# Closing attention's buffer pools one stage earlier, and making the block products' input sums there

## The chip, the cores and the metric

The kernel runs on one core of a Trainium2 chip. The metric is the device time of one execution in microseconds (us), as the median over several executions. The engines are TensorE (PE, with its weight loads listed as PEld), VectorE (DVE), ScalarE (ACT), GpSimd (POOL) and SyncE (SP), which issues nearly all DMAs.

## The reference

Three stages follow each other. q, k, v have shape (4, 12, 448, 64): four batches, twelve heads.

```python
q_n, k_n = rmsnorm(q, g_q), rmsnorm(k, g_k)
attn = softmax(q_n @ k_n.T / 8)          # per batch and head, 448 x 448
x = (attn @ v)                           # as 1792 tokens x 768
h = x @ moe_w_in;  g = s * relu(h)**2 + b;  x = g @ moe_w_out      # 768 -> 2048 -> 768
h = x @ moe2_w_in; out = (h * cos(h)) @ moe2_w_out                 # 768 -> 2048 -> 768
```

The weights of the first layer come as float64 and the result is float32, so the products are made in three passes from pairs of a high and a low part.

## The kernel before

**Tiling.** A matrix is held as a pair: `high` is a cast to fp32r made by ACT, `low` is the remainder, one subtraction made by DVE or POOL. Each product is three matmuls: high by high, high by low, low by high (`products`, L138). A batch is 448 columns. The hidden dimension of 2048 is cut into eight chunks of two 128-row tiles.

**Order of the work.** The two feed-forward layers are one list of units, made at L887 to L925. An `in` unit makes one 128 x 448 tile of h (18 matmuls) and its activation; an `out` unit adds one chunk's share to one output tile (6 matmuls), after which DVE adds it to the accumulator (L801), or ACT copies it at a tile's first visit (L799). The first layer goes through segments: 0 and 2 are chunk 0 for batch 0 and for batch 1, 1 is chunks 1 to 7 for batches 0 and 1, and 3 (the second pass) is all eight chunks for batches 2 and 3. Segment 4 is the second layer. A generator, `attention` (L149), is advanced between the units by a planner of costs (L1003 to L1008). A scheduler then orders each engine's queue: earlier in the program goes first among what it takes to be ready, and only written dependences bind. `issue_after` (L107) fixes an order in a queue without a wait, `follow` (L103) is a wait.

**Block products.** From chunk 2 of segment 3 on, the `in` work of a chunk is one unit `seven` (L668): seven products of half size in place of eight. It needs sums of blocks of the inputs (t1 to t4) and of the weights (`load_combined`, L588). For each of three columns c, `fetch_x` (L621) reads four 128 x 448 pieces of attention's result back from DRAM, and `combine_x` (L628) makes four differences on DVE (L630 to L633), four high casts on ACT (L636) and four low parts on DVE (L637). They stand in segment 3: fetches behind its 1st, 3rd and 5th following unit, sums behind the 4th, 6th and 9th (L988 and L989). The first fetch of each column follows a high cast of a recent `in` unit (L626), and the first difference is queued behind a recent activation on DVE (L630).

**Memory.** Attention has an SBUF pool `att` and a PSUM pool `ps` of six banks (`sc` four, `tp` two); two more banks, tag `mo`, are the feed-forward's own. At the end of segment 2 (L980 to L987) `att` and `ps` are closed and their room goes to `xb` (the second home of inputs), `mb` (among others eight buffers `acc`) and the PSUM pool `psb` (three banks `ph` for `in`, three banks `po` for `out`). Until then `in` units take `mo` and `out` units take `mo`, or `sc` once all pairs are finished (`po_tile`, L775). `fetch` (L860) reads batch 3 back into six tiles of `att`.

**Names of time.** The change's point is the unit `in` of segment 1, chunk 7, tile 0, batch 1. Counted from it: 0 and 1 are that `in` and the next, 3 and 4 the two `in` units of segment 2, 5 to 16 the `out` units of chunk 7, 17 to 22 those of segment 2, 23 is the border to segment 3, 24 to 29 are six `in` units, and 30 is its first `out`.

Of the kernel before, what the change touches and what calls it, by code (L numbers as in the profile page):

```python
# [10 lines left out]
F32 = mybir.dt.float32  # L11
# [4 lines left out]
ALU = mybir.AluOpType  # L16
AX = mybir.AxisListType
PSUM = bass.MemoryType.PSUM
# [25 lines left out]
def body(ctx, tc, q, k, v, g_q, g_k, w1_in, w1_out, s_in, b_in, w2_in, w2_out, out):  # L44
# [23 lines left out]
    LOOK = 8  # L68
    TAIL = 14
    NEAR = 4  # L70
    AHEAD = 3, 5
    SEVEN = 2

    const = ctx.enter_context(tc.tile_pool(name="const", bufs=1))
    dram = ctx.enter_context(tc.tile_pool(name="dram", bufs=1, space=DRAM))
# [544 lines left out]

    def fetch_x(c):  # L621
        x11, x12, x21, x22 = mixed["raw", c] = [pools["mb"].tile([P, E], F32, tag="acc", name=f"xc_{c}_{n}", bufs=2 * NT - NE)[:, :S] for n in range(4)]
        for n, (t, b, cc) in enumerate(((x11, 2, c), (x12, 3, c), (x22, 3, c + NE // 2), (x21, 2, c + NE // 2))):
            dma = nc.sync.dma_start(t, stash[0, b, cc])
            if n == 0:
                follow(dma, marks["gh"])  # L626

    def combine_x(c):  # L628
        x11, x12, x21, x22 = mixed.pop(("raw", c))
        issue_after(nc.vector.tensor_tensor(x11, x12, x11, ALU.subtract), marks["sums"])  # L630
        nc.vector.tensor_tensor(x12, x22, x12, ALU.subtract)
        nc.vector.tensor_tensor(x22, x22, x11, ALU.subtract)
        nc.vector.tensor_tensor(x21, x21, x22, ALU.subtract)  # L633
        for n, (name, t) in enumerate((("t1", x11), ("t3", x12), ("t2", x22), ("t4", x21))):
            hi, lo = mixed[name, c] = [z[:, n // 2 * S:(n // 2 + 1) * S] for z in held_x["b"][c + n % 2 * (NE // 2)]]
# [8 lines left out]
    def g_pair(key, seg):  # L644
        n = count["pairs"] % (5 if seg > 3 else 4)
        count["pairs"] += 1
        if "mb" not in pools or n < 3:
            gp, tag, nb = ma, "g", 3
        else:
            gp, tag, nb = pools["mb"], "gx"[n - 3], 1  # L650
        return [gp.tile([P, 2 * S], F32R, tag=tag + z, name=f"g{z}_{key}", bufs=nb) for z in "hl"]

    def squared(h, key, place=None):
        def temp(pool, tag, name):
            return pool.tile([P, WIDE], F32, tag=tag, name=f"{name}_{key}")[:, :h.shape[1]]

        r = temp(ma, "t0", "r") if place is None else place
        nc.scalar.activation(r, h, AF.Relu)
        r2 = temp(pools["mb"], "t1", "r2") if "mb" in pools else r
# [5 lines left out]
        marks["sums"] = nc.vector.tensor_scalar(gt, r2, sb[:, 0:1], sb[:, 1:2], ALU.mult, ALU.add)  # L665
        return gt

    def unit_seven(layer, seg, ck, *_):  # L668
# [115 lines left out]
    def unit_out_1(seg, ck, et, b):  # L784
# [73 lines left out]
    early = {}  # L858

    def fetch(b):  # L860
        for c in range(NP):
            t = pools["att"].tile([P, S], F32, tag=("xf", "qT", "kT")[c % 3], name=f"xe_{b}_{c}")
            nc.sync.dma_start(t, stash[0, b, c])
            early[0, b, c] = t

    def behind_weights(high, low, eng):
        near = [z for z in casts if z[0] <= count["unit"] + NEAR]
# [71 lines left out]

    def lead(z):  # L940
        n, key = z
        return n - AHEAD[key[1] > SEVEN] if key[0] == "s" else n

    todo.sort(key=lead)

# [19 lines left out]
    enter = [units.index(("next", seg)) for seg in range(1, L2 + 1)]  # L965
    last = {max(n for n, u in enumerate(units) if u[:3] == ("in", 0, 1) and u[5] == 0): 2, enter[2] - TAIL: 3}
    rates = [1.05 * PAIR * (2 * NP - ALONE) / spent(units[:enter[0]]), 1.05 * PAIR * 2 * NP / spent(units[enter[0]:max(last)])]
    debt = 0.0
    seg = 0
    soon, again = [], []  # L970
    fetches, sums = {}, {}
    wait = 0
    for n, u in enumerate(units):
        count["unit"] = n
        ahead(n + LOOK)
        if u[0] == "next":
            seg = u[1]
            if seg == 1:
                until(2)
            if seg == 3:  # L980
                for _ in steps:
                    pass
                att_scope.close()
                pools["xb"] = ctx.enter_context(tc.tile_pool(name="xb", bufs=1))
                held_x["b"] = paired(pools["xb"], "b")
                pools["mb"] = ctx.enter_context(tc.tile_pool(name="mb", bufs=2))
                pools["psb"] = ctx.enter_context(tc.tile_pool(name="psb", bufs=2, space=PSUM))  # L987
# [14 lines left out]
        for cost in {"in": unit_in, "seven": unit_seven, "out": unit_out}[u[0]](*u[1:]):  # L1002
            debt += cost * rates[min(seg, 1)]  # L1003
            while debt > 0:
# [1 line left out]
                if c is None:  # L1006
                    break
                debt -= c  # L1008
        if n in fetches:
            fetch_x(fetches[n])  # L1010
        if n in sums:
            combine_x(sums[n])
# [36 lines left out]
```

## Time and profile before

| what | value |
|---|---|
| median of 3 executions | 1248.81 us (1247.53 to 1249.16) |
| profiled execution, its own time | 1248.98 us |
| its span, first to last instruction | 1247.2 us |
| mean granted TensorE clock | 0.998 |
| PE, DVE, ACT, POOL busy | 98%, 72%, 62%, 49% |

A row of the waits says which engine sat idle, for which instruction, and what ended the idle time. In a timeline the idle time before an instruction and its releaser stand in brackets at the end of its row. Matmuls overlap their neighbours, so their starts tell the pace: products of 448 columns follow each other by about 0.2 us.

### The profile page before, as it was taken

Reading aid. Unit: us, or ns where it says so; the run is one execution under the profiler, and the core shown is the slowest. Engines: PE = TensorE matmul, PEld = TensorE weight load, DVE = VectorE, ACT = ScalarE, POOL = GpSimd, SP = SyncE. Lnnn points to the kernel's source line nnn. Section 1 sums busy time; section 2 is a strip of 40 time slices with the busy share of each in tenths; the row PEclk is TensorE's granted clock in tenths of the full one; section 3 lists DMA queues with packets and bytes.
Section 4 is the critical chain, followed back from the end, with each engine's and each line's share of the span. In section 5 each row is a group of like instructions: output and inputs, shape, how many; then the busy total and the mean of one; then the engine's idle time right before and its main releaser. Section 6 shows DMA issues by size and latency. Waiting matters only on the chain.

```text
span 1247.2 us, 18906 instructions
## 1 busy us (share of the span) xinstructions
PE 1220.1 (98%) x6575; PEld 1032.8 (83%) x6575; DVE 893.5 (72%) x1510; ACT 777.6 (62%) x1725; POOL 608.3 (49%) x724
## 2 busy tenths in 40 slices
PE   7999999999999999999999999999999999999998
PEld 5555777777777877888898988899999999999997
DVE  6888778767768664758777778575777666676765
ACT  4788888776666663536445446698666756565640
POOL 4777647464544524734333333556444635363541
PEclk9999999999999999999999999999999999999999
DMA  4334336344333333443212241131111111111105
GB/s 119 96 106 119 106 97 196 111 134 132 116 114 106 113 122 121 158 155 93 58 51 69 78 139 42 36 114 52 52 51 52 51 52 51 51 52 51 55 10 177
DMA packets 88463, 114.08 MB, mean 91 GB/s; under 512 B 11952, under 2 KB 78512, under 8 KB 88368
## 3 DMA queue, kind: packets, MB, share of 16 engines
q1 hardware_dynamic: 88048, 112.66, 29.7%
q8 instruction: 51, 0.84, 0.3%
q14 instruction: 44, 0.36, 0.1%
q10 hardware_dynamic: 320, 0.23, 0.1%
HBM read 89.26 MB, written 23.59 MB: 90 GB/s over the span
## 4 chain that ended last, share of the span: by engine, by line
PE 71%; DVE 5%; ACT 2%; DMA 2%; issue 1%; POOL 1%; SPq 0%; DVEq 0%; ACTq 0%; POOLq 0%
PE ph L741 25%; PE po L819 18%; PE po L793 14%; PE av L407 3%; PE tp L372 3%; PE ph_s L685 3%; PE sc L320 3%; PE ph_a L685 2%; DMA t<-wd 1%; DVE xlb L127 0%; DVE xlb L637 0%; DVE acc L801 0%; ACT wh L535 0%; PE rt L391 0%; DVE wl L538 0%
## 5 line engine op out<-in xcount | busy, mean ns | idle before, releaser
L765 POOL TENSOR_TENSOR gl<-gt,gh 128x512 fp32r<-128x512 f32 (+1 forms) x104 | 126.6, 1228 | 119.4 <-ACT gh L764 119.2
L538 POOL TENSOR_TENSOR wl<-t,wh 128x384 fp32r<-128x384 f32 x128 | 140.3, 1112 | 90.1 <-ACT wh L535 82.6
L741 PE MATMUL ph<-xha,wh 128*128 128x448 f32 (+2 forms) x432 | 159.6, 370 | 1.5 <-DVE acc L801 0.8
L741 PE MATMUL ph<-xha,wl 128*128 128x448 f32 (+2 forms) x432 | 158.2, 366 | 0.0
L741 PE MATMUL ph<-xla,wh 128*128 128x448 f32 (+2 forms) x432 | 157.5, 366 | 0.0
L819 PE MATMUL po<-wh,gh 128*128 128x384 f32 x448 | 151.9, 340 | 1.3 <-DVE acc L827 1.3
L827 DVE TENSOR_TENSOR acc<-po,acc 128x384 f32<-128x384 f32 x196 | 105.5, 551 | 64.9 <-PE po L819 64.6
L819 PE MATMUL po<-wh,gl 128*128 128x384 f32 x448 | 150.0, 335 | 0.0
L819 PE MATMUL po<-wl,gh 128*128 128x384 f32 x448 | 149.5, 335 | 0.0
L801 DVE TENSOR_TENSOR acc<-po,acc 128x448 f32<-128x448 f32 (+2 forms) x168 | 102.0, 618 | 49.7 <-PE po L793 48.9
L763 POOL TENSOR_TENSOR gt<-hs,gt 128x512 f32<-128x512 f32 x64 | 76.8, 1206 | 119.2 <-ACT gt L762 118.8
L535 ACT CAST wh<-t 128x384 fp32r<-128x384 f32 x176 | 84.2, 512 | 70.6 <-PE po L793 27.5
L579 DVE SCALAR_TENSOR_TENSOR t<-c,t 128x384 uint32<-128x384 uint32 x128 | 96.4, 755 | 40.2 <-ACT t L573 36.8
L347 ACT ACTIVATE pr<-sc,top 128x448 f32<-128x448 f32 x161 | 102.3, 640 | 17.0 <-DVE top L335 16.4
L335 DVE TENSOR_REDUCE top<-sc 128x1 f32<-128x448 f32 x168 | 98.3, 616 | 15.7 <-PE sc L320 14.9
L572 ACT ACTIVATE c<-raw 128x384 f32<-128x384 f32 x128 | 71.2, 558 | 52.3 <-DMA raw<-in_moe_w_in_dram 17.3
L793 PE MATMUL po<-gh,wh 128*128 128x448 f32 (+1 forms) x240 | 91.7, 387 | 6.8 <-DVE acc L801 3.7
L372 PE MATMUL tp<-ident,pr 128*112 128x128 f32 x672 | 95.3, 278 | 1.1 <-DVE pT L384 0.5
L372 PEld LDWEIGHTS tp<-ident,pr 128*112 128x112 f32 x672 | 74.6, 134 | 24.9 <-issue 13.3
L764 ACT CAST gh<-gt 128x512 fp32r<-128x512 f32 (+1 forms) x104 | 57.8, 567 | 56.5 <-DVE gt L665 29.1
L741 PEld LDWEIGHTS ph<-xha,wh 128*128 128x128 f32 x432 | 81.1, 188 | 13.0 <-issue 2.2
L819 PEld LDWEIGHTS po<-wh,gh 128*128 128x128 f32 x448 | 84.1, 188 | 8.9 <-DVE acc L827 6.0
(181 smaller groups left out, 3161.7 us busy)
## 6 DMA issues: line engine op xcount, KB each, us to landing
raw<-in_moe_w_in_dram SPq DMA_DIRECT2D x64, 384.0 KB, 3.6
raw<-in_moe_w_out_dram SPq DMA_DIRECT2D x64, 384.0 KB, 3.3
wd<-t SPq DMA_DIRECT2D x64, 192.0 KB, 2.7
t<-wd SPq DMA_DIRECT2D x48, 192.0 KB, 2.4
rawk<-in_k_dram SPq DMA_DIRECT2D x24, 224.0 KB, 2.9
rawv<-in_v_dram SPq DMA_DIRECT2D x24, 224.0 KB, 3.1
rs<-wd SPq DMA_DIRECT2D x24, 192.0 KB, 2.7
rawq<-in_q_dram SPq DMA_DIRECT2D x23, 192.0 KB, 2.9
```

Source lines behind the costliest of these rows:

```text
L335: line("DVE", nc.vector.tensor_reduce(top, st[i]["sc", c][j][1][:, :S], axis=AX.X, op=ALU.max, negate=True))
L347: e = line("ACT", nc.scalar.activation(pr, sc[:, :S], AF.Exp, bias=st[i]["top"][:, at], scale=scale, accum_out=st[i]["sums"][:, at]))
L372: mm = [nc.tensor.transpose(tp[:, kc * P:(kc + 1) * P], pr[:, kc * CP:(kc + 1) * CP], ident) for kc in range(NCH)]
L535: z = nc.scalar.copy(wh, w)
L538: casts.append((count["needed"], z, eng, eng.tensor_tensor(wl, w, wh.bitcast(F32), ALU.subtract)))
L579: nc.vector.scalar_tensor_tensor(t, c, 0x80000000, t, ALU.bitwise_and, ALU.bitwise_or)
L741: nc.tensor.matmul(h, a, m, start=(c == 0 and n == 0), stop=(c == NE - 1 and n == 2))
L765: nc.gpsimd.tensor_tensor(gl, gt, gh.bitcast(F32), ALU.subtract)
L793: marks["out"] = nc.tensor.matmul(po, a, m, start=(f == 0 and n == 0), stop=(f == CF - 1 and n == 2))
L801: nc.vector.tensor_tensor(at, po, at, ALU.add)
L819: nc.tensor.matmul(po, a, m, start=(f == 0 and n == 0), stop=(f == CF - 1 and n == 2))
L827: nc.vector.tensor_tensor(at, po, at, ALU.add)
```

## The change

Both pools are closed in front of unit 0 instead of at the border to segment 3. `fetch` reads batch 3 into three wide tiles of `mb`. `combine_x` is split into `sums_x` (differences and high casts) and `lows_x` (low parts, two of four now on POOL), and the three steps of column c come behind the units in `PREPARE`, counted from the change's point. The wait of the first fetch on a high cast goes. The order mark is also set by each accumulation. The weight sums of chunk 2 are asked for five units ahead instead of three. Pairs of g before segment 3 stay in their old pool.

```diff
-    AHEAD = 3, 5
+    AHEAD = 5
+    PREPARE = (0, 3, 6), (1, 10, 14), (16, 25, 27)
...
     def fetch_x(c):
...
-            dma = nc.sync.dma_start(t, stash[0, b, cc])
-            if n == 0:
-                follow(dma, marks["gh"])
-    def combine_x(c):
-        x11, x12, x21, x22 = mixed.pop(("raw", c))
-        issue_after(nc.vector.tensor_tensor(x11, x12, x11, ALU.subtract), marks["sums"])
+            nc.sync.dma_start(t, stash[0, b, cc])
+    def sums_x(c):
+        x11, x12, x21, x22 = mixed["raw", c]
+        issue_after(nc.vector.tensor_tensor(x11, x12, x11, ALU.subtract), marks["DVE"])
...
             nc.scalar.copy(hi, t)
-            nc.vector.tensor_tensor(lo, t, hi.bitcast(F32), ALU.subtract)
+    def lows_x(c):
+        x11, x12, x21, x22 = mixed.pop(("raw", c))
+        for n, (name, t) in enumerate((("t1", x11), ("t3", x12), ("t2", x22), ("t4", x21))):
+            hi, lo = mixed[name, c]
+            z = (nc.vector if n % 2 else nc.gpsimd).tensor_tensor(lo, t, hi.bitcast(F32), ALU.subtract)
+            if n == 1:
+                issue_after(z, marks["DVE"])
...
-        nc.vector.tensor_tensor(at, po, at, ALU.add)
+        marks["DVE"] = nc.vector.tensor_tensor(at, po, at, ALU.add)
...
     def fetch(b):
-            t = pools["att"].tile([P, S], F32, tag=("xf", "qT", "kT")[c % 3], name=f"xe_{b}_{c}")
+        for n, tag in enumerate(("xh", "xl", "gh")):
+            t = pools["mb"].tile([P, 2 * S], F32, tag=tag, name=f"xe_{b}_{n}", bufs=1)
...
+    change = units.index(("in", 0, 1, NCK - 1, 0, 1))
...
-            if seg == 3:
-                for _ in steps:
-                    pass
-                att_scope.close()
...
-                fetches = {n + 1: 0, n + 3: 1, n + 5: 2}
-                sums = {n + 4: 0, n + 6: 1, n + 9: 2}
+        if n == change:
+            until(B)
+            for _ in steps:
+                pass
+            att_scope.close()
+            pools["xb"] = ctx.enter_context(tc.tile_pool(name="xb", bufs=1))
...
+        for step, c in prepare.get(n, ()):
+            step(c)
```

## Rows read from the trace of the kernel before

**Rows 1.** The page: busy time by engine, and the chain by engine.
```profile
PE 1220.1 (98%) x6575; PEld 1032.8 (83%) x6575; DVE 893.5 (72%) x1510; ACT 777.6 (62%) x1725; POOL 608.3 (49%) x724
PE 71%; DVE 5%; ACT 2%; DMA 2%; issue 1%; POOL 1%; SPq 0%; DVEq 0%; ACTq 0%; POOLq 0%
```
**Rows 2.** Waits of PE, 490 to 600 us: total, times, longest.
```profile
PE po L793 <- ACT acc L799: 2.5, 3, 1.5
...
PE po L793 <- DVE acc L801: 0.6, 1, 0.6
```
**Rows 3.** PE's timeline around the change: start, us, instruction, idle before.
```profile
487.75 3.23 PE L407 MATMUL av<-pT,rawv 112*64 112x448 f32 x16
...
500.49 0.36 PE L741 MATMUL ph<-xha,wh 128*128 128x448 f32 x1
...
538.84 0.44 PE L741 MATMUL ph<-xha,wh 128*128 128x448 f32 x1 [0.81 <-DVE acc L801]
...
571.14 0.47 PE L793 MATMUL po<-gh,wh 128*128 128x448 f32 x1 [1.48 <-ACT acc L799]
...
613.71 0.44 PE L793 MATMUL po<-gh,wh 128*128 128x384 f32 x1 [1.51 <-DVE acc L801]
```
**Rows 4.** ACT's timeline at the longest of those waits.
```profile
564.65 0.56 ACT L636 CAST xhb<-xc 128x448 fp32r<-128x448 f32 x1 [2.13 <-DVE xc L633]
565.12 0.53 ACT L799 COPY acc<-po 128x448 f32<-128x448 f32 x1
...
570.09 0.56 ACT L636 CAST xhb<-xc 128x448 fp32r<-128x448 f32 x1 [0.79 <-DVE xc L632]
570.56 0.53 ACT L799 COPY acc<-po 128x448 f32<-128x448 f32 x1
```
**Rows 5.** Stretches: length, then busy time of PE, PEld, DVE, ACT, POOL.
```profile
516.00:538.84 22.84, 21.43 (x106) 19.12 (x104) 18.45 (x29) 8.86 (x20) 13.86 (x12) 1.00 0.60 198
538.84:561.10 22.26, 22.26 (x109) 20.15 (x110) 10.48 (x17) 7.66 (x16) 9.43 (x9) 1.00 0.41 128
...
529.86:543.51 13.65, 12.84 (x64) 11.52 (x63) 7.45 (x14) 3.33 (x7) 0.01 (x2) 1.00 0.60 206
```
**Rows 6.** Groups by shape, 538.84 to 588.3 us: busy, mean ns, idle before.
```profile
L637 DVE TENSOR_TENSOR xlb<-xc,xhb 128x448 fp32r<-128x448 f32 x12 | 9.5, 803 | 0.0
...
L632 DVE TENSOR_TENSOR xc<-xc,xc 128x448 f32<-128x448 f32 x3 | 4.2, 1409 | 0.1
L631 DVE TENSOR_TENSOR xc<-xc,xc 128x448 f32<-128x448 f32 x3 | 2.8, 944 | 0.0
L633 DVE TENSOR_TENSOR xc<-xc,xc 128x448 f32<-128x448 f32 x3 | 2.5, 850 | 0.0
...
L630 DVE TENSOR_TENSOR xc<-xc,xc 128x448 f32<-128x448 f32 x3 | 1.8, 613 | 0.0
...
L636 ACT CAST xhb<-xc 128x448 fp32r<-128x448 f32 x12 | 6.8, 568 | 5.1 <-DVE xc L632 2.3 <-DVE xc L633 2.1 <-DVE xc L631 0.6
```
**Rows 7.** DVE's timeline: accumulations ahead of unit 0, an activation behind unit 3.
```profile
497.85 3.46 DVE L801 TENSOR_TENSOR acc<-po,acc 128x448 f32<-128x448 f32 x6 [4.79 <-PE po L793]
...
516.39 1.33 DVE L665 TENSOR_SCALAR gt<-r,sb 128x448 f32<-128x448 f32 x1 [0.83 <-POOL r L661]
```
**Rows 8.** Groups of DVE, 516 to 538.84 us: low parts of weights.
```profile
L538 DVE TENSOR_TENSOR wl<-t,wh 128x384 fp32r<-128x384 f32 x9 | 6.7, 785 | 0.9 <-ACT wh L535 0.9
```
**Rows 9.** POOL's low parts of batch 3, 500.49 to 538.84 us.
```profile
L127 POOL TENSOR_TENSOR xla<-xe,xha 128x448 fp32r<-128x448 f32 x6 | 7.6, 1289 | 0.0
```
**Rows 10.** The twelve reads of attention's result: the line's DMA.
```profile
DMA to landing us min/median/max: 2.5/3.3/5.2
```
**Rows 11.** Timelines of DVE and POOL at the first differences.
```profile
559.41 0.61 DVE L631 TENSOR_TENSOR xc<-xc,xc 128x448 f32<-128x448 f32 x1
560.06 1.47 DVE L632 TENSOR_TENSOR xc<-xc,xc 128x448 f32<-128x448 f32 x1
...
559.16 1.88 POOL L765 TENSOR_TENSOR gl<-gt,gh 128x448 fp32r<-128x448 f32 x1 [1.98 <-ACT gh L764]
```

More of the change, by code (lines that the diff above doesn't have):

```diff
@@ L622, in fetch_x @@
         x11, x12, x21, x22 = mixed["raw", c] = [pools["mb"].tile([P, E], F32, tag="acc", name=f"xc_{c}_{n}", bufs=2 * NT - NE)[:, :S] for n in range(4)]
-        for n, (t, b, cc) in enumerate(((x11, 2, c), (x12, 3, c), (x22, 3, c + NE // 2), (x21, 2, c + NE // 2))):
-            dma = nc.sync.dma_start(t, stash[0, b, cc])
-            if n == 0:
-                follow(dma, marks["gh"])
-    def combine_x(c):
-        x11, x12, x21, x22 = mixed.pop(("raw", c))
-        issue_after(nc.vector.tensor_tensor(x11, x12, x11, ALU.subtract), marks["sums"])
+        for t, b, cc in (((x11, 2, c), (x12, 3, c), (x22, 3, c + NE // 2), (x21, 2, c + NE // 2))):
+            nc.sync.dma_start(t, stash[0, b, cc])
+    def sums_x(c):
+        x11, x12, x21, x22 = mixed["raw", c]
+        issue_after(nc.vector.tensor_tensor(x11, x12, x11, ALU.subtract), marks["DVE"])
         nc.vector.tensor_tensor(x12, x22, x12, ALU.subtract)
@@ L634, in combine_x @@
         for n, (name, t) in enumerate((("t1", x11), ("t3", x12), ("t2", x22), ("t4", x21))):
-            hi, lo = mixed[name, c] = [z[:, n // 2 * S:(n // 2 + 1) * S] for z in held_x["b"][c + n % 2 * (NE // 2)]]
+            hi, _ = mixed[name, c] = [z[:, n // 2 * S:(n // 2 + 1) * S] for z in held_x["b"][c + n % 2 * (NE // 2)]]
             nc.scalar.copy(hi, t)
-            nc.vector.tensor_tensor(lo, t, hi.bitcast(F32), ALU.subtract)
+    def lows_x(c):
[5 more added lines that the diff above has]
+                issue_after(z, marks["DVE"])
     g = {}
@@ L646, in g_pair @@
         count["pairs"] += 1
-        if "mb" not in pools or n < 3:
+        if seg < 3:
+            n = 0
+        if n < 3:
             gp, tag, nb = ma, "g", 3
@@ L664, in squared @@
         gt = temp(ma, "t2", "gt")
-        marks["sums"] = nc.vector.tensor_scalar(gt, r2, sb[:, 0:1], sb[:, 1:2], ALU.mult, ALU.add)
+        marks["DVE"] = nc.vector.tensor_scalar(gt, r2, sb[:, 0:1], sb[:, 1:2], ALU.mult, ALU.add)
         return gt
@@ L860, in fetch @@
     def fetch(b):
-        for c in range(NP):
-            t = pools["att"].tile([P, S], F32, tag=("xf", "qT", "kT")[c % 3], name=f"xe_{b}_{c}")
-            nc.sync.dma_start(t, stash[0, b, c])
-            early[0, b, c] = t
+        for n, tag in enumerate(("xh", "xl", "gh")):
+            t = pools["mb"].tile([P, 2 * S], F32, tag=tag, name=f"xe_{b}_{n}", bufs=1)
+            for c in (2 * n, 2 * n + 1):
+                at = t[:, c % 2 * S:(c % 2 + 1) * S]
+                nc.sync.dma_start(at, stash[0, b, c])
+                early[0, b, c] = at
     def behind_weights(high, low, eng):
@@ L941, in lead @@
         n, key = z
-        return n - AHEAD[key[1] > SEVEN] if key[0] == "s" else n
+        return n - AHEAD if key[0] == "s" else n
     todo.sort(key=lead)
@@ L967, in body @@
     rates = [1.05 * PAIR * (2 * NP - ALONE) / spent(units[:enter[0]]), 1.05 * PAIR * 2 * NP / spent(units[enter[0]:max(last)])]
+    change = units.index(("in", 0, 1, NCK - 1, 0, 1))
+    prepare = {}
+    for c, times in enumerate(PREPARE):
+        for step, at in zip((fetch_x, sums_x, lows_x), times):
+            prepare.setdefault(change + at, []).append((step, c))
     debt = 0.0
@@ L970, in body @@
     soon, again = [], []
-    fetches, sums = {}, {}
     wait = 0
@@ L979, in body @@
                 until(2)
-            if seg == 3:
-                for _ in steps:
-                    pass
-                att_scope.close()
[L984 to L987, printed above, removed]
-                fetches = {n + 1: 0, n + 3: 1, n + 5: 2}
-                sums = {n + 4: 0, n + 6: 1, n + 9: 2}
-            continue
+            continue
+        if n == change:
[4 more added lines that the diff above has]
+            pools["xb"] = ctx.enter_context(tc.tile_pool(name="xb", bufs=1))
+            held_x["b"] = paired(pools["xb"], "b")
+            pools["mb"] = ctx.enter_context(tc.tile_pool(name="mb", bufs=2))
+            pools["psb"] = ctx.enter_context(tc.tile_pool(name="psb", bufs=2, space=PSUM))
         if wait:
@@ L1008, in body @@
                 debt -= c
[L1009 to L1012, printed above, removed]
+        for step, c in prepare.get(n, ()):
+            step(c)
         if u[0] == "seven" and u[3] == NCK - 1:
```

## The prediction, made before the changed kernel was run

> **What bounds the kernel now.** I read the page first, then PE's waits around the change, the timelines at those waits, and a table of stretches. PE is busy in 1220.1 us of a span of 1247.2 us and carries 71% of the chain that ends last [rows 1]. So a gain can only come out of PE's 27 us of idle time, and a loss is new idle time. Between 490 and 600 us the waits of PE that the change could touch are few: 2.5 us in three waits for ACT's copies of a first visit, 0.6 us once for an accumulation on DVE [rows 2], and 0.81 us in front of the first `in` of segment 3 at 538.84 us [rows 3]. Another 1.51 us stands at 613.71 us [rows 3]. Nothing behind that belongs to the sums.
>
> The 2.5 us have a cause that the reader can see in ACT's queue. The copy at 565.12 us, which gives a PSUM bank back to PE, is queued behind a high cast of a sum that had waited 2.13 us for a difference on DVE. At 570.56 us it is the same: the cast ahead had waited 0.79 us [rows 4]. PE's longest wait, 1.48 us, ends right behind that second copy, at 571.14 us [rows 3]. So the input sums, where they stand now, hold PE up by way of ACT's order.
>
> **The change part by part.** The sum is made against the profiled execution, whose own time is 1248.98 us (span 1247.2 us and 1.8 us around it); the median of three is 1248.81 us, 0.2 us less, so I carry the difference over to the median.
>
> *The pools close at unit 0.* Attention is not in the way: its last product starts at 487.75 us and takes 3.23 us, and unit 0 starts at 500.49 us [rows 3]. Nothing is left to drain, so running the generator dry costs nothing; if pairs were left there, their sixteen products alone would cost 3.2 us each. But the new PSUM pool takes the room of banks that the last `out` units still use. Before, the first tile of that pool waited 0.81 us at 538.84 us, until the last accumulation was done [rows 3]. That wait goes, and its like comes at unit 0: six accumulations run from 497.85 to 501.31 us [rows 7], and the tile that now starts at 500.49 us would start at 501.31 us at the earliest, +0.8 us. If the bank in question is free sooner, it is nothing. The wait at 538.84 us is the nearest row, so I take +0.8 us and keep 0.
>
> *Columns 0 and 1 move into the `out` units.* Their first difference is queued behind the activation of unit 3, which DVE makes at 516.39 us [rows 7], so this work lies where DVE gives PE its banks back. In 516.00 to 538.84 us, DVE is busy 18.45 us of 22.84 us and PE 21.43 us [rows 5]. What is added on DVE is eight differences and four low parts. At the shortest of them, 0.61 us [rows 6], that is 7.4 us. At the means, the four differences have 0.61, 0.94, 1.41 and 0.85 us, 3.8 us a column, and two low parts 2 x 0.80 us [rows 6]: 5.4 us a column and 10.8 us in all. What need not be done before the last `out` product: three accumulations, since three banks of the new pool can stay full (3.46 / 6 = 0.58 us each [rows 7], 1.7 us); column 1's low parts, which the block products read only after 577 us; and low parts of weights that segment 3 uses, two of the nine at 0.78 us [rows 8], 1.6 us.
>
> Bounds: PE's own 21.43 us if DVE never holds it up, which is 1.4 us less than now (it contains the waits of 0.60 and 0.81 us). With all twelve at their means and only the accumulations put off, 18.45 + 10.8 - 1.7 = 27.6 us, 4.7 us more. I take column 0 at its mean, 5.4 us, because POOL works through all of its 13.86 us before 529.86 us, and column 1's four differences short, 2.4 us, because POOL then is idle (0.01 us of 13.65 us [rows 5]); one of the two weight parts, 0.8 us, is put off: 18.45 + 7.8 - 1.7 - 0.8 = 23.75 us, +0.9 us.
>
> The long rows decide this term. A difference took 1.47 us while POOL made a low part, yet the one ahead of it, under the same POOL instruction, took 0.61 us [rows 11]; so POOL's work stretches some of them. The Trainium skill, "SBUF — State Buffer", section "Who interferes with whom", has a rule that speaks against this change: a DVE instruction with two SBUF inputs and a GpSimd instruction that reads SBUF contend, and the second to issue blocks fully. By that rule, with the 1.41 us of L632 for all six of column 0, the term would be 3.1 us larger and the sum +2.3 us; the trace agrees in one of the two rows and not in the other.
>
> *The old place is emptied.* In 538.84 to 588.3 us eight of twelve casts, 0.57 us each, and all but four differences and two low parts leave ACT and DVE [rows 6]. Column 2 stays, but its differences now come behind unit 25 and its low parts behind unit 27, where DVE is busy 10.48 us of 22.26 us [rows 5]: 5.4 us fit. If that cover were gone, one cast wait of 0.79 us as in rows 4 would come back. I take -2.5 us for the three waits; the other end is -0.8 us, if two thirds of it stay. The wait of 1.51 us at 613.71 us belongs to the next weight sums; I take nothing for it, with -1.5 us as the end.
>
> *Costed at nothing.* Twelve reads leave the stretch behind 545 us for one before it; they land in 3.3 us [rows 10], and nobody but the differences waits for them; if they were late, DVE's queue and the accumulations behind would stand for as long. They pass weight reads on SP's queue, which are issued eight units ahead. Four low parts at 1.29 us [rows 9], 5.2 us, go to POOL before segment 3 and two later; the 13.65 us that POOL stands idle hide the four [rows 5]. What POOL owes before that are g's low parts, needed by the `out` units of segment 2. Eight casts, 4.5 us, go to ACT, busy 8.86 us of 22.84 us [rows 5]. The reads of batch 3 go to tiles of the new pool, so they can start once the last result is in DRAM, an estimate of 494 us (attention's last product ends at 490.98 us [rows 3], and a transfer lands in about 3 us [rows 10]); their splits on POOL run till 529.86 us, and PE wants them behind 538.84 us. Asking for chunk 2's weight sums two units earlier adds no work. The scratch buffer for raw weights that goes with attention's pool has two loads left to serve.
>
> Sum: +0.8 + 0.9 - 2.5 = -0.8 us, so 1248.2 us as profiled and **1248.0 us** as a median.
>
> **The rivals.** *The sums slip in between the accumulations (faster).* The stretch then takes PE's 21.43 us (-1.4), the old waits go (-2.5), the gate costs 0 to 0.8 us, and the wait at 613.71 us may go too (-1.5): -3.1 to -5.4 us, about -3.9 us or 1244.9 us. For it speaks that DVE has 6.2 us idle between 529.86 and 543.51 us [rows 5]; against it, that a difference chain comes in one piece and is earlier in the program than the accumulations behind it.
>
> *DVE becomes the bound of the `out` stretch (slower).* One mechanism: with three banks instead of four, accumulations queue behind four differences in a row, stretched by POOL, and PE has no bank. Its place is units 5 to 22, its price 4.7 us, with the gate +0.8 and the gain -2.5: +3.0 us, 1251.8 us. It decides from where the twelve instructions take more than 10.3 us together, 0.86 us each: 18.45 + 10.3 - 1.7 is 4.2 us above 22.84 us, and the sum then +2.5 us. For it speaks the 0.6 us that PE waited for DVE there already [rows 2]. It is the outcome that the rule of the blocked port in the Trainium skill, "SBUF — State Buffer", gives.
>
> *ACT's copies stay late.* The weight sums of chunk 2 move up into the space that the input sums leave, and two thirds of the 2.5 us remain: +0.8 + 0.9 - 0.8 = +0.9 us, 1249.7 us. Against it speak the releasers of the casts, all differences [rows 4, 6].
>
> **How the numbers follow.** A measurement of this kernel can tell about 0.2%, 2.5 us, from no change. I give the forecast 0.42, the faster rival 0.33, the slower one 0.20, the late copies 0.05. The forecast's own range is 1246.5 to 1250.3 us. All of the faster rival is over 2.5 us, and with 0.02 from the forecast's low end faster gets 0.35; slower gets 0.20 and 0.02; same 0.43. The range runs from 1244.4 us, past the middle of the faster rival, to 1251.6 us, just short of the slower one's price.
>
> **What would show it.** Right: PE waits under 1 us for accumulations in front of unit 0's first product, has no wait for ACT's first-visit copies, and DVE has hardly a gap through the `out` units, with PE waits for L801 of 1 to 3 us there. The stretch from unit 5's first product to segment 3's takes 23 to 25 us. Wrong: no PE wait in that stretch (then the first rival), or over 4 us of them (the second); copies on ACT still behind waiting casts (the third). A wait of PE on attention at unit 0 would overturn the first part.

## The result: 12 us slower

| | before | after |
|---|---|---|
| median of 4 executions | 1248.99 us (1247.53 to 1249.26) | 1260.64 us (1259.87 to 1261.34) |
| profiled execution, its own time (span) | 1248.98 us (1247.2) | 1261.34 us (1259.6) |
| mean granted TensorE clock | 0.998 | 0.993 |

The ratio is 1.0096, with a 95% interval of 1.0078 to 1.0113: slower by 11.7 us. The forecast was 1248.0 us, and the range ended at 1251.6 us. The rival on the slower side comes nearest, at a quarter of the size.

### The profile page after: what moved, and what is told of

Same layout as the page of the kernel before. It is cut to its first block, busy times and chain, and to the rows that moved or that the text cites. A ratio compares the mean times of both kernels' runs of the same rounds, so it can differ in the third digit from the quotient of the medians.

```text
span 1259.6 us, 18889 instructions
## 1 busy us (share of the span) xinstructions
PE 1225.4 (97%) x6575; PEld 1035.0 (82%) x6575; DVE 900.1 (71%) x1504; ACT 778.8 (62%) x1725; POOL 615.6 (49%) x730
## 4 chain that ended last, share of the span: by engine, by line
PE 73%; DVE 4%; ACT 2%; POOL 2%; issue 1%; DMA 1%; SPq 0%; DVEq 0%; ACTq 0%; POOLq 0%
PE ph L749 25%; PE po L827 18%; PE po L801 16%; PE ph_s L693 3%; PE av L408 3%; PE tp L373 3%; PE sc L321 3%; PE ph_a L693 2%; DVE t L580 1%; DVE wl L539 0%; POOL gl L773 0%; DVE xlb L128 0%; POOL r L669 0%; DMA xr<-xd 0%; PE rt L392 0%
## 5 line engine op out<-in xcount | busy, mean ns | idle before, releaser
L580 DVE SCALAR_TENSOR_TENSOR t<-c,t 128x384 uint32<-128x384 uint32 x128 | 96.6, 757 | 40.2 <-ACT t L574 36.7
L801 PE MATMUL po<-gh,wh 128*128 128x448 f32 (+2 forms) x240 | 93.9, 394 | 11.7 <-DVE acc L809 7.2
L749 PEld LDWEIGHTS ph<-xha,wh 128*128 128x128 f32 x432 | 81.2, 188 | 13.8 <-issue 2.2
L581 DVE SCALAR_TENSOR_TENSOR t<-c,t 128x384 uint32<-128x384 uint32 x128 | 90.3, 708 | 1.9
```

Source lines behind the costliest of these rows:

```text
L580: nc.vector.scalar_tensor_tensor(t, c, 0x80000000, t, ALU.bitwise_and, ALU.bitwise_or)
L581: nc.vector.scalar_tensor_tensor(t, c, 3, t, ALU.logical_shift_left, ALU.bitwise_or)
L749: nc.tensor.matmul(h, a, m, start=(c == 0 and n == 0), stop=(c == NE - 1 and n == 2))
L801: marks["out"] = nc.tensor.matmul(po, a, m, start=(f == 0 and n == 0), stop=(f == CF - 1 and n == 2))
```

## The profile after

First the page of the changed kernel: the busy times, then the chain by engine, against [rows 1].

```profile
PE 1225.4 (97%) x6575; PEld 1035.0 (82%) x6575; DVE 900.1 (71%) x1504; ACT 778.8 (62%) x1725; POOL 615.6 (49%) x730
...
PE 73%; DVE 4%; ACT 2%; POOL 2%; issue 1%; DMA 1%; SPq 0%; DVEq 0%; ACTq 0%; POOLq 0%
```

The page finds nothing: PE has 5.3 us more of busy time for the same 6575 products, and the engines' shares stand almost as before. What changed shows in the stretch. Here are PE's waits between 490 and 640 us (total, times, longest), against [rows 2].

```profile
PE po L801 <- DVE acc L809: 6.2, 1, 6.2
PE po L801 <- ACT acc L807: 2.8, 1, 2.8
...
```

One wait of 6.2 us for an accumulation is new. Two timelines show where the wait lies and what follows it: DVE's row ahead of unit 0, against [rows 7], and then PE's rows, against [rows 3].

```profile
497.59 3.46 DVE L809 TENSOR_TENSOR acc<-po,acc 128x448 f32<-128x448 f32 x6 [4.78 <-PE po L801]
```
```profile
500.40 0.47 PE L749 MATMUL ph<-xha,wh 128*128 128x448 f32 x1
...
515.09 0.36 PE L801 MATMUL po<-gh,wh 128*128 128x448 f32 x1
...
518.80 0.47 PE L801 MATMUL po<-gh,wh 128*128 128x448 f32 x1 [0.71 <-ACT gh L772]
...
520.31 0.47 PE L801 MATMUL po<-gl,wh 128*128 128x448 f32 x1 [0.64 <-POOL gl L773]
526.95 0.74 PE L801 MATMUL po<-gh,wh 128*128 128x448 f32 x1 [6.17 <-DVE acc L809]
527.49 0.57 PE L801 MATMUL po<-gh,wl 128*128 128x448 f32 x1
...
531.60 0.53 PE L801 MATMUL po<-gh,wh 128*128 128x448 f32 x1
531.96 0.37 PE L801 MATMUL po<-gh,wl 128*128 128x448 f32 x1
```

Read it from the top. The six accumulations ahead of unit 0 end at 501.05 us. PE starts unit 0's first product at 500.40 us, with no wait in brackets: the gate that the new PSUM pool was thought to be did not close. The `out` units begin at 515.09 us; three of them fill the three banks, and after the product at 520.31 us PE stands still until 526.95 us. Then the products start 0.37 us apart instead of 0.20 us, up to 531.60 us.

DVE's timeline says what it did meanwhile.

```profile
516.95 2.31 DVE L673 TENSOR_SCALAR gt<-r,sb 128x448 f32<-128x448 f32 x2
519.18 1.56 DVE L629 TENSOR_TENSOR xc<-xc,xc 128x448 f32<-128x448 f32 x1
520.77 1.44 DVE L630 TENSOR_TENSOR xc<-xc,xc 128x448 f32<-128x448 f32 x1
522.25 1.43 DVE L631 TENSOR_TENSOR xc<-xc,xc 128x448 f32<-128x448 f32 x1
523.71 1.24 DVE L632 TENSOR_TENSOR xc<-xc,xc 128x448 f32<-128x448 f32 x1
524.88 1.48 DVE L539 TENSOR_TENSOR wl<-t,wh 128x384 fp32r<-128x384 f32 x1
526.28 0.61 DVE L809 TENSOR_TENSOR acc<-po,acc 128x448 f32<-128x448 f32 x1
```

No row has idle time in brackets. Column 0's four differences take 5.7 us in one piece, a low part of weights follows, and only then comes the first accumulation, 5.5 us after the last product that PE could place ended. Counted from unit 0's first product it comes at 25.9 us; before, at 17.2 us, by this row of its trace.

```profile
517.64 0.61 DVE L801 TENSOR_TENSOR acc<-po,acc 128x448 f32<-128x448 f32 x1
```

The table of stretches (length, busy time of PE, PEld, DVE, ACT, POOL, then the granted clock) gives the clock beside it.

```profile
520.00:525.00 5.00, 0.47 (x1) 0.19 (x1) 4.90 (x5) 3.26 (x7) 5.00 (x5) 0.67 0.19 60
525.00:530.00 5.00, 3.05 (x8) 2.75 (x9) 5.00 (x6) 1.56 (x4) 4.88 (x4) 0.50 0.46 123
```

The granted clock stands at 0.50, the 1.2 GHz level, behind the wait. Before, it was 1.00 in both stretches. POOL is busy throughout the differences, 5.00 of 5.00 us.

How late is PE at which point? Both kernels do the same products, so the start of the product at which a given number of columns is done can be subtracted. At 500 us the two stand within 0.3 us. From there on PE is 10.4 us later at 550 us, 14.3 us at 600 us, 11.5 us at 660 us, and 12.2 us at the end. The 10.4 us can be summed from the starts: 8.1 us in the three waits with brackets above (each start against the start due), 2.2 us in 13 products at 0.37 us, some 2 us in shorter stops up to 543 us where column 1's differences alternate with the accumulations and at restarts, less the 2 us or so that before lost there itself.

The second loss lies at 577 to 583 us: ACT's rows, PE's, and then the rows of SP's DMA issues and of its waits.

```profile
581.88 0.51 ACT L536 CAST wh<-t 128x384 fp32r<-128x384 f32 x1 [4.94 <-DMA t<-wd]
582.29 0.53 ACT L807 COPY acc<-po 128x448 f32<-128x448 f32 x1
```
```profile
576.99 0.68 PE L749 MATMUL ph<-xha,wh 128*128 128x512 f32 x2 [1.33 <-ACT wh L536]
...
582.87 0.54 PE L801 MATMUL po<-gh,wh 128*128 128x448 f32 x1 [2.84 <-ACT acc L807]
```
```profile
576.89 1.64 SPq L595 DMA_DIRECT2D rs<-wd  x3
578.64 0.36 SPq L553 DMA_DIRECT2D t<-wd  x1
```

And from the waits of SP's queue, 560 to 590 us:

```profile
SPq L595 <- DVE wsl L605: 5.2, 2, 4.8
```

It has the form of [rows 4], ACT's copy behind a cast that waits, with another releaser: a read of weights. That read was issued at 578.64 us, behind reads `rs` for weight sums, which SP's queue held until 576.89 us, 4.8 us long, for a low part of weight sums on DVE (L605). DVE itself was busy in 15.47 of the 15.51 us from 564.20 to 579.71 us. So the old waits of 2.5 us for differences are gone, and 4.2 us of new ones stand near their place. From 600 to 660 us 2.8 us come back: the wait of before at 613.71 us [rows 3] is absent, and so is this one, from PE's timeline of before.

```profile
603.82 0.45 PE L793 MATMUL po<-gh,wh 128*128 128x384 f32 x1 [0.57 <-DVE acc L801]
```

## The experiments

The tables give the median of this kernel and of the one before on the same chip, the ratio with its interval, and how much later PE stands than before at 550 us, at 600 us and at the end, each counted from 500 us (starts at equal columns, as above). In the expectations, theory A is that the block of four differences stands ahead of the accumulations, B that closing early costs the time and B' that its three PSUM banks instead of four do, C that the amount of DVE's work in those units decides, D that late accumulations and late low parts of g do. E and F are on the second loss: E that the reads and buffers of the weight sums cause it, F that DVE and POOL are late with column 2 and all else.

| kernel | this | before | ratio | PE later at 550, 600, end |
|---|---|---|---|---|
| the change itself | 1260.64 | 1248.99 | 1.0096 [1.0078, 1.0113] | 10.4, 14.3, 12.2 |
| e1, old places | 1253.59 | 1247.40 | 1.0052 [1.0037, 1.0067] | 3.2, 6.6, 5.2 |
| e2, column 0 at unit 0 | 1258.19 | 1247.40 | 1.0089 [1.0074, 1.0104] | 7.3, 11.2, 9.3 |
| e3, and column 1 late | 1260.88 | 1247.40 | 1.0106 [1.0091, 1.0121] | 8.1, 15.3, 12.9 |
| e4, five banks | 1258.91 | 1247.40 | 1.0084 [1.0067, 1.0101] | 8.9, 15.5, 13.2 |
| e5, old places, five banks | 1250.72 | 1248.32 | 1.0022 [1.0013, 1.0032] | -0.8, 2.5, 1.7 |
| e6, old places, three raw buffers | 1252.78 | 1248.32 | 1.0044 [1.0027, 1.0060] | 2.6, 6.1, 4.7 |
| e7, the old lead | 1260.18 | 1248.32 | 1.0096 [1.0081, 1.0111] | 9.7, 13.8, 11.4 |
| e8, differences on POOL | 1253.25 | 1248.32 | 1.0042 [1.0027, 1.0057] | 3.7, 8.5, 6.5 |
| e9, the same, five banks | 1251.65 | 1247.54 | 1.0035 [1.0023, 1.0048] | 0.3, 7.4, 5.1 |
| e10, two columns on POOL, five banks | 1252.01 | 1247.54 | 1.0033 [1.0022, 1.0045] | -0.6, 6.0, 3.4 |
| e11, and column 2 late | 1248.46 | 1247.67 | 1.0002 [0.9993, 1.0011] | 0.3, 3.1, 1.3 |
| e12, and the old lead | 1248.29 | 1247.67 | 1.0005 [0.9996, 1.0014] | 1.9, 4.4, 2.3 |

The profiles are of one execution each, and the last column goes by them: the profiled execution stands up to 1.4 us beside its kernel's median in most, 2.1 us above it in e12 and 3.0 us above it in e4.

### Old places: the early closing alone (e1)

The pools close at unit 0, and the sums stand where they were. The rest of the change stays: the longer lead, half of the low parts on POOL, batch 3 in wide tiles.

```diff
-    PREPARE = (0, 3, 6), (1, 10, 14), (16, 25, 27)
+    PREPARE = (24, 27, 27), (26, 29, 29), (28, 32, 32)
```

> The changed kernel with the sums of all three columns back in segment 3, where the kernel before had them (fetches behind units 24, 26, 28, sums and low parts behind 27, 29, 32); the pools still close at unit 0, so out units still have three PSUM banks instead of four. Theory A (column 0's four differences stand in one piece ahead of the first accumulations, and PE has no bank): the wait of 6.2 us and the drop of the granted clock behind it are gone, and the time comes back to that of the kernel before, 1248 to 1252 us, with ACT's waits for the first-visit copies back (about 2.5 us). Theory B (closing early, that is three banks or the new pool's first tiles, costs the time): at least half of the loss stays, 1255 us or more.

PE's waits of this kernel, 490 to 600 us, and a stretch:

```profile
PE po L801 <- ACT acc L807: 4.6, 4, 2.0
PE po L801 <- DVE acc L809: 1.6, 1, 1.6
```
```profile
520.00:525.00 5.00, 4.89 (x18) 4.43 (x19) 4.25 (x7) 1.32 (x3) 5.00 (x5) 0.70 0.56 170
```

Early closing, with that rest, costs 6.2 us by the medians, about half the loss, so neither theory's range held: 3.2 us up to 550 us, one wait for an accumulation of 1.6 us and seven slow products behind it among them. DVE makes the first accumulation 21.4 us behind unit 0's first product, here at 498.04 us:

```profile
519.45 0.61 DVE L809 TENSOR_TENSOR acc<-po,acc 128x448 f32<-128x448 f32 x1
```

So of the 8.7 us by which it is later in the change than before, 4.3 us come without any sum in these units. The old waits for ACT's copies are back, and larger (4.6 us against 2.5 us in [rows 2]).

### Column 0 at unit 0 (e2, e3)

Column 0's sums are queued behind the last accumulation ahead of unit 0, so that nothing of theirs is in front of the accumulations of the `out` units; e3 puts column 1 behind the border to segment 3 besides.

```diff
-    PREPARE = (0, 3, 6), (1, 10, 14), (16, 25, 27)
+    PREPARE = (0, 0, 3), (1, 10, 14), (16, 25, 27)
...
+            marks["close"] = marks["DVE"]
...
-        issue_after(nc.vector.tensor_tensor(x11, x12, x11, ALU.subtract), marks["DVE"])
+        issue_after(nc.vector.tensor_tensor(x11, x12, x11, ALU.subtract), marks["DVE" if c else "close"])
```

In e3 the first line has `(1, 24, 26)` for column 1.

> The changed kernel with column 0's sums behind unit 0 and queued right behind the accumulations ahead of unit 0, its low parts behind unit 3; columns 1 and 2 as in the change. The same DVE work, only column 0's seven to ten us earlier, while in units run that need no bank from DVE. Theory A (place in the queue): the 6.2 us wait and the clock's drop vanish, 8 to 10 us less than the changed kernel, 1250 to 1253 us. Theory C (DVE has too much work between 500 and 545 us, wherever it stands): the accumulations are late by as much, some shorter waits of PE take the place of the long one, 1255 us or more.

> As the run before, and column 1's sums and low parts behind units 24 and 26, so that no difference stands among the out units of segments 1 and 2. Theory A: as the run before, 1250 to 1253 us, since column 1's differences alternate with accumulations and cost PE nothing; the second loss of about 4 us around 577 to 588 us stays. Theory C: 3 us or more below the run before.

PE's wait in e2, and DVE's rows ahead of its end:

```profile
525.04 0.74 PE L801 MATMUL po<-gh,wh 128*128 128x448 f32 x1 [4.38 <-DVE acc L809]
```
```profile
519.22 1.33 DVE L580 SCALAR_TENSOR_TENSOR t<-c,t 128x384 uint32<-128x384 uint32 x1
...
523.04 1.41 DVE L539 TENSOR_TENSOR wl<-t,wh 128x384 fp32r<-128x384 f32 x1 [0.94 <-ACT wh L536]
524.37 0.61 DVE L809 TENSOR_TENSOR acc<-po,acc 128x448 f32<-128x448 f32 x1
```

The differences are gone from the place and 4.4 of the 6.2 us of waiting stay. Now the conversions of weights (L579 to L581), which column 0's sums have pushed back, stand there, and behind them a low part that waits for its cast. Theory A falls in its strict form: it isn't the four differences as such that must stand last. Without column 1 in the `out` units (e3) the wait is the same, and the loss behind 550 us is larger. e3 was to gain 3 us or more by theory C as well, and it is 2.7 us slower than e2: the amount of DVE's work in these units alone doesn't decide either.

### Banks (e4, e5)

Two banks that stand idle in these units (tag `mo`) take two of every five `out` tiles before segment 3, so accumulations have five banks. e4 is the change with this, e5 is e1 with this.

```diff
-        if "psb" in pools:
+        count["po"] = count.get("po", 0) + ("psb" in pools)
+        if "psb" in pools and not (seg < 3 and count["po"] % 5 > 2):
...
-        elif finished["pairs"] == B * NP:
+        elif "psb" not in pools and finished["pairs"] == B * NP:
```

> The changed kernel with two more PSUM banks for the out units between the change and segment 3 (the two idle banks mo, in turn with the three of the new pool): five instead of three. Theory A with the banks as a buffer: two more out units (2.4 us) pass ahead of the wait, which shrinks from 6.2 to about 3.7 us; 1256 to 1258 us, and less if the clock then doesn't drop. Theory B (three banks instead of four are the cause): the loss of the first stretch is gone, 1250 to 1252 us.

> The run with the sums at their old places and early closing, plus the two idle PSUM banks for the out units between the change and segment 3. That run is about 6 us slower than the kernel before, with a wait of 1.6 us for an accumulation at 520 us and two of 0.5 and 0.6 us before it, and longer waits for ACT at 567 to 578 us. Theory B' (three banks are what early closing costs in the out units): the 1.6 us wait goes, 2 to 3 us less, 1250 to 1251.5 us. Theory D (late accumulations and g's low parts cost it, since DVE's and POOL's queues in front of them are longer): less than 1 us changes.

PE's waits of e4, then of e5 with the stretch that answers to the one shown of e1:

```profile
PE po L802 <- DVE acc L810: 6.2, 2, 4.7
```
```profile
PE po L802 <- ACT acc L808: 3.5, 3, 2.0
```
```profile
520.00:525.00 5.00, 4.91 (x25) 4.04 (x24) 5.00 (x9) 3.58 (x9) 5.00 (x5) 1.00 0.67 203
```

With the sums at their old places, five banks remove every wait for an accumulation up to 600 us: 4.0 us of the first stretch (3.2 to -0.8 us) and 3.8 us of the median come back, all that early closing cost in the `out` units. Whether the loss of one bank was the cause isn't shown by this, for five is one more than before had, and they also cover accumulations that come late: in e5 the first still comes 21.0 us behind unit 0's first product. With the sums in the `out` units the same banks take off 1.5 us of 10.4 us in that stretch and nothing at the end, by a profile that is 3.0 us above the median; the medians give 11.5 us in place of 11.7 us. e4 missed both ranges. PE fills the banks, and waits 4.7 and 1.5 us. Banks cover a late accumulation once; they don't make DVE's work less.

### Buffers of raw weights, and the lead of the weight sums (e6, e7)

e6 is e1 with a third buffer for raw weights; e7 is the change with chunk 2's sums asked for three units ahead, as before.

```diff
-            raw = (wp if own else pools["att"]).tile([P, CW], I64, tag="raw", name=f"raw_{kk}", bufs=2 if own else 1)
+            if own or "mb" not in pools:
+                raw = (wp if own else pools["att"]).tile([P, CW], I64, tag="raw", name=f"raw_{kk}", bufs=2 if own else 1)
+            else:
+                raw = pools["mb"].tile([P, CW], I64, tag="acc", name=f"raw_{kk}", bufs=2 * NT - NE)
```
```diff
-    AHEAD = 5
+    AHEAD = 3, 5
```

> The run with the sums at their old places and early closing, and a third buffer again for the raw weights of segment 1's last chunk (closing the pool early leaves two, so that their conversions on DVE come later and stand directly ahead of the activations and accumulations of the next units). Theory D: the conversions are off DVE earlier, the waits at 516 to 520 us shrink, 1.5 to 3 us less. Theory B': no change there.

> The changed kernel with the weight sums of chunk 2 asked for three units ahead again, as in the kernel before, instead of five. Theory E (the second loss, PE waiting 1.3 us for a weight's cast and 2.8 us for ACT at 577 to 583 us, comes from the weight sums' reads and buffers standing ahead of the weight reads): 3 to 5 us less, 1255 to 1258 us. Theory F (it comes from DVE and POOL being late with column 2 and all else): no change, 1259 to 1261 us.

Neither moves the time by more than its interval. In e6 PE's wait for an accumulation falls from 1.6 to 0.5 us, as theory D had it, but the one for a low part of g grows from 0.6 to 1.3 us, and 0.6 us of the first stretch come back. In e7 the waits of 6.2, 3.0 and 1.3 us stand where the change has them; the lead is cleared of the loss at 577 us, which I had suspected it of. That the time stays is what F forecast, but no run takes column 2 alone away, so F isn't shown.

### The differences on POOL (e8 to e10)

All twelve differences go to POOL, behind its last low part of batch 3 (L128), where POOL then stood idle [rows 5]. The place moves with the engine: columns 0 and 1 come behind units 18 and 20 instead of 3 and 10, their low parts behind 20 and 22. In e9 the banks are five, all low parts are DVE's, and the places are `(0, 18, 20), (1, 19, 21), (20, 22, 25)`; in e10, with e8's places and five banks, column 2's differences are DVE's again, and half of the low parts are POOL's as in the change.

```diff
-    PREPARE = (0, 3, 6), (1, 10, 14), (16, 25, 27)
+    PREPARE = (0, 18, 20), (1, 20, 22), (21, 25, 27)
...
+        if eng is nc.gpsimd:
+            marks["POOL"] = low
...
-        issue_after(nc.vector.tensor_tensor(x11, x12, x11, ALU.subtract), marks["DVE"])
+        issue_after(nc.gpsimd.tensor_tensor(x11, x12, x11, ALU.subtract), marks["POOL"])
```

> The changed kernel with the differences on POOL instead of DVE, queued behind the last low part of batch 3: columns 0 and 1 behind units 18 and 20, column 2's behind 25; low parts behind 20, 22 and 27, half on each engine as in the change. Theory C (DVE is the bound of the out units; every us of differences there is a us of PE): DVE is rid of some 13 us of differences, the wait of 6.2 us and the clock's drop go, and the first stretch loses only what early closing costs: 1252 to 1255 us. Were it a matter of when the sums are ready or of the early closing alone, it would stay near 1260 us.

> Theory: three things made the change slow, VectorE's differences ahead of the first accumulations (about 7 us), three banks instead of four (about 3 us), and late weight sums at 565 to 590 (about 2). Here no difference is on VectorE in the out units and the banks are five, so the first stretch should stand at 550 us as it did with the old places and five banks (1 to 2 us ahead of before), with no wait of TensorE over 1 us for an accumulation of VectorE; with ScalarE's old waits of 2.5 us absent the time is 1245 to 1247 us. Rival: GpSimd, which holds the differences, is late with the residuals and low parts of the chunk's own path (3.9 us at 572 when all differences stood on it with three banks); then ph or g waits for GpSimd by 3 us or more between 565 and 580 and the time is 1249 to 1252.

> Columns 0 and 1's differences on GpSimd, column 2's on VectorE, five banks. Theory: the first stretch as with old places and five banks, no wait for VectorE's accumulations over 1 us; GpSimd has four differences fewer than with all on it, so its wait at 567 to 573 falls below 2 us: 1246 to 1249 us. Rival (the late weight sums at 577 to 583 are the issue order of the weight loads on SyncE's queue, not GpSimd): waits for wh and ScalarE's copies of 3 us or more remain there, 1250 to 1252.

PE's waits of e8, 490 to 600 us:

```profile
PE po L803 <- ACT gh L774: 4.9, 2, 3.9
...
PE po L803 <- DVE acc L811: 1.6, 1, 1.6
```

With three banks, no difference on DVE and its low parts only from 542.70 us on, the wait for accumulations is e1's 1.6 us, and the first stretch costs e1's 3 to 4 us instead of 10.4 us. So 6.7 us of the first stretch (10.4 - 3.7), and 6.7 us of the medians, are the sums in DVE's queue at units 3 to 14. That POOL makes them isn't what counts there: e1, with all differences on DVE but later, comes to the same (10.4 - 3.2 = 7.2 us). With five banks as well (e9, e10) that stretch costs nothing. But both lose 6 to 7 us behind 550 us. e9's time is its rival's, with PE waiting 4.7 us for `gh` and 2.0 us for `gl`. In e10 theory and rival both missed: the wait for a copy, the rival's sign, is 0.9 us. The timelines of e10 show what stands in the way, first POOL's, then DVE's:

```profile
555.72 1.25 POOL L672 TENSOR_TENSOR r<-r 128x448 f32<-128x448 f32 x1
...
561.64 1.31 POOL L607 TENSOR_TENSOR wsl<-ts,wsh 128x384 fp32r<-128x384 f32 x1
562.92 1.44 POOL L776 TENSOR_TENSOR gl<-gt,gh 128x448 fp32r<-128x448 f32 x1
```

```profile
556.09 1.35 DVE L635 TENSOR_TENSOR xc<-xc,xc 128x448 f32<-128x448 f32 x1
557.37 1.50 DVE L541 TENSOR_TENSOR wl<-t,wh 128x384 fp32r<-128x384 f32 x1
...
559.92 0.51 DVE L676 TENSOR_SCALAR gt<-r,sb 128x448 f32<-128x448 f32 x1
```

The chunk's own path goes through POOL twice, for the square (L672) and for g's low part (L776), and between them through DVE for `gt` (L676); low parts of the sums and of the weight sums (L607) stand between on POOL. PE waits 1.96 us for that `gl` and 4.2 us for `gh`. The longest of the waits for `gh`, 1.88 us at 561.78 us, is more DVE's than POOL's: the square is done at 556.97 us, and its `gt` starts 2.95 us later, behind column 2's last difference, low parts and a weight sum.

### Column 2 late (e11, e12)

e11 is e10 with column 2 near its old place and all low parts on DVE (and columns 0 and 1 up to a unit earlier); e12 is e11 with the old lead of the weight sums.

```diff
-    PREPARE = (0, 18, 20), (1, 20, 22), (21, 25, 27)
+    PREPARE = (0, 18, 19), (1, 19, 21), (26, 29, 31)
...
-            z = (nc.vector if n % 2 else nc.gpsimd).tensor_tensor(lo, t, hi.bitcast(F32), ALU.subtract)
+            z = nc.vector.tensor_tensor(lo, t, hi.bitcast(F32), ALU.subtract)
```

> Five banks, columns 0 and 1's differences on GpSimd in the hole that it had between 530 and 543 us, all low parts on VectorE, column 2 whole on VectorE near its old place (behind unit 29). Theory: the loss of the two kernels before at 560 to 571 us was GpSimd's low parts and differences standing in front of the residuals and g's low parts of segment 3's chunk 1; with none of them on GpSimd behind 543 us, the first stretch stays 2 us ahead of before and no wait for gl or gh over 1 us comes at 560 to 575; ScalarE has 4 casts there instead of 12, so its waits stay under 1.5 us: 1244.5 to 1247 us. Rival: the loss at 560 to 571 is the weight sums, asked for five units ahead instead of three (their casts and sums stand before g's casts on ScalarE); then the waits for gh of 1.7 us and more stay: 1249 to 1251 us.

> The same with chunk 2's weight sums asked for three units ahead, as before the change. If GpSimd's order was the cause, this is the kernel above within 1 us; if the lead was, the waits for gh and gl at 560 to 571 go here and not above: 1244.5 to 1247 us against 1249 or more.

PE's waits of e11, 490 to 640 us:

```profile
PE po L805 <- ACT gh L775: 2.6, 2, 2.0
...
PE po L805 <- POOL gl L776: 0.5, 1, 0.5
```

The wait for `gl` falls from 2.0 to 0.5 us, and of the 6.6 us that e10 loses between 550 and 600 us, 2.8 us remain. The time can't be told from that of before, so the ranges of theory and rival both missed. POOL's low parts and column 2's place changed together, and DVE's `gt` waited for column 2 in e10, so how much of the 3.8 us was POOL's order isn't shown. The lead is cleared a second time (e12 doesn't beat e11). The theory's gain of 1 to 3 us didn't come, for a wait for `gh` of 2.0 us stayed, the rival's sign; with the old lead it is still 1.8 us. The trace of e11 shows what stands on its path: its ACT `r` is done at 558.53 us, POOL's square starts at 560.72 us behind low parts of weight sums (L607) and a `gl`, and DVE's `gt` at 562.89 us behind two steps of weight sums (L611, L618). Of the kernels tried none is faster than before.

## Why the prediction was wrong

**The step that failed** is "Columns 0 and 1 move into the `out` units", the term of +0.9 us. It measured 10.4 us with all that hung on it, of which e8 puts 6.7 us on the differences and low parts of these columns in DVE's queue, and e1 and e5 about 4.0 us on early closing with three banks. The two shares are not a sum: with the sums in place, two more banks took off 1.5 us. Three things in the term's working were off.

- *Durations.* I took column 0 at its mean, column 1's differences short, 7.8 us for what had to be done, and had 10.8 us as the high end. The twelve instructions took 13.2 us, 9.4 for the differences and 3.9 for the low parts, added up from unrounded durations: here are the longest and the shortest of the four lines of differences and the low parts, from DVE's groups of the changed kernel, 516 to 546.8 us (busy, mean ns).

```profile
L641 DVE TENSOR_TENSOR xlb<-xc,xhb 128x448 fp32r<-128x448 f32 x4 | 3.8, 964 | 0.0
...
L630 DVE TENSOR_TENSOR xc<-xc,xc 128x448 f32<-128x448 f32 x2 | 2.5, 1235 | 0.0
...
L629 DVE TENSOR_TENSOR xc<-xc,xc 128x448 f32<-128x448 f32 x2 | 2.2, 1086 | 0.0
```

  The means of [rows 6] came from a place where POOL is idle for stretches. Beside column 0 in the new place POOL worked without a gap, and all four of its differences were long, 1.24 to 1.56 us. The rule that the prediction weighed, in the Trainium skill, "SBUF — State Buffer", section "Who interferes with whom", fits the new place in four rows of four; [rows 11], with one of two, made me leave it to the slower rival. Column 1's four, 0.61 to 1.04 us, came out at the mean and not short. With 13.2 us the sum's own high end is 18.45 + 13.2 - 1.7 = 29.95 us, +7.1 us in place of +4.7 us.
- *No order in the sum.* It added DVE's work up over 22.84 us, as if an accumulation could go ahead of a difference whenever PE needed a bank. The rows show the order kept: the first accumulation starts behind all that was queued ahead of it, and PE stood idle for 6.2 us. e3 shows best what such a sum can't see: with no difference in these units PE still loses 8.1 us up to 550 us, while DVE is idle for 8.7 us. But order isn't the whole. Here are the stretches from 516 us until PE has done the columns that before had done at 539.1 us, in the change, e4 and e3 (length, then PE, PEld, DVE, ACT, POOL):

```profile
516.11:549.29 33.18, 25.51 (x106) 20.89 (x104) 30.81 (x41) 14.33 (x30) 21.50 (x16) 0.85 0.51 159
```
```profile
516.45:547.78 31.33, 24.07 (x105) 20.37 (x104) 31.19 (x40) 13.79 (x28) 21.93 (x16) 0.95 0.45 147
```
```profile
515.53:546.05 30.52, 24.37 (x105) 21.17 (x104) 21.84 (x32) 9.76 (x21) 16.59 (x15) 0.89 0.56 182
```

  In the change DVE is idle for 2.4 of 33.2 us, and with five banks, which cover a late accumulation, for 0.1 of 31.3 us. So the amount was too much as well. The runs don't separate how much of the 10.4 us is order and how much amount.
- *The clock.* No term was there for it. Behind the idle time the granted clock was 0.50, and 13 products took 0.17 us longer each, 2.2 us by the starts. Whether these are a loss of their own isn't shown: from 516 to 547 us DVE had a single pause, 0.72 us that end at 533.18 us, so a faster PE might have waited for DVE instead. In [rows 3] the waits were 1.5 us and less, and the products behind the one at 571.14 us followed at 0.2 us, so the profile of before showed no price for a long one.

**The banks.** They stood in the slower rival, inside its price; the term itself used the three banks only to put accumulations off. e1 and e5 show that about 4 us can be lost and won by them even with no sum moved, since early closing makes the first accumulation 4.3 us later by itself. Why it does is open. The scratch buffer for raw weights, which the prediction costed at nothing, accounts for little: e6 gives a buffer back and gains 0.6 us of that stretch. The row of 0.6 us in [rows 2], with four banks, was the sign: DVE was late there already.

**The gate at unit 0** was predicted at +0.8 us and cost 0: PE starts at 500.40 us while the accumulations run to 501.05 us. The text allowed for it ("if the bank in question is free sooner").

**The old place emptied, -2.5 us.** The three waits for copies behind casts of differences are gone as said. What the step lacked is what came late next: 4.2 us at 577 to 583 us, behind the weight sums' reads on SP's queue. The prediction said of the inputs' reads that "They pass weight reads on SP's queue", and costed that at nothing; it never asked about the weight sums' own buffers, nor whether DVE would free them in time. The end of the range at -1.5 us for the wait at 613.71 us did come true: with the one at 603.82 us, 2.8 us by the starts.

**The slower rival** was right in place and sign, and in the main in its mechanism: the three banks by e5, the work on DVE by e1 and e8, the stretching beside POOL by the rows. "Four differences in a row" is what e2 doesn't bear out as a condition, since 4.4 us of the wait stayed without them. Its price of 4.7 us is too small for the reasons above. The over 4 us of PE waits that the text named as its sign is what stands in the trace.

**What stays open.** The 2.0 us for `gh` in e11 is followed only in the trace, and the second loss, 577 to 583 us in the change, wasn't taken apart: e7 clears the lead, e6 tried a buffer for the ordinary weights, none was tried for the sums' own. No run has the differences of columns 0 and 1 on DVE behind unit 18, which would tell the engine from the place in e8.

## What to carry to other kernels

When work moves onto an engine that also frees another's buffers, don't only weigh it against that engine's idle time over the stretch: write its queue out in order as well, and sum what stands ahead of the first instruction that frees a buffer, against the buffers that are left. Take the durations from a stretch where the neighbouring engine is as busy as in the new place. And look at the granted clock behind a long wait of PE: here 13 products behind it took 0.17 us longer each.

## What was not expected of the hardware

- Behind 6.17 us without a product the granted clock fell to 0.50 (1.2 GHz of 2.4), and 13 products started 0.37 us apart in place of 0.20 us; behind the 2.84 us that end at 582.87 us the next ones did as well (583.21, 583.59, 583.96 us). The length of the last wait alone doesn't tell: behind 1.57 us in e1 (520.11 us), with 0.48 and 0.63 us of idle time shortly before, seven products started 0.37 us apart; behind 2.00 us in e11 (564.05 us) they kept 0.20 us.
- Two engines slow each other. In e10 POOL's differences took 1.13 us each at 529.84 us, where DVE had two accumulations from PSUM and else was idle, and 1.53 us at 537.15 us, beside DVE's low parts; DVE's in the change took 0.61 us at 533.72 us, with POOL idle, and 1.24 to 1.56 us beside it. The timeline of POOL in e10:

```profile
529.84 2.26 POOL L632 TENSOR_TENSOR xc<-xc,xc 128x448 f32<-128x448 f32 x2
...
537.15 3.07 POOL L634 TENSOR_TENSOR xc<-xc,xc 128x448 f32<-128x448 f32 x2
```
